# Moving a chunk's last scores and statistics up among the PV matmuls, and filling TensorE's wait for the next keys with unused matmuls

## The chip, the cores and the metric

One core of one Trainium2 chip (trn2). The metric is the device time of one execution in microseconds. Nearly everything here is a matter of one or two microseconds in 1386, so times are given as medians with all runs' range, and differences only where kernels ran in the same rounds on the same chip.

## The reference

Two decode attentions of one query token, batch 4, 32 query heads, head size 128, bf16. A is grouped (8 key heads) over the last 2048 positions; B has 32 key heads and reads all 8192.

```python
def _B_ref(x, k_cache, v_cache, wq, wo):                 # k_cache, v_cache: (4, 32, 8192, 128)
    q = (x @ wq).reshape(B, Sq, H, Dh).transpose(0, 2, 1, 3)
    scores = jnp.einsum("bhqd,bhkd->bhqk", q, k_cache) * (Dh ** -0.5)
    p = _softmax(scores, axis=-1)
    o = jnp.einsum("bhqk,bhkd->bhqd", p, v_cache)
    return o.transpose(0, 2, 1, 3).reshape(B, Sq, H * Dh) @ wo
# A the same on k_cache[:, :, Sk - W:], W = 2048, heads repeated 4 times; the results are concatenated
```

Each key and value is used once: 587 MB have to come from HBM.

## The kernel before

The work is cut into 72 chunks: 8 of A, then 64 of B ("second-half chunks"; 4 MB of keys and 4 MB of values each). For each chunk TensorE transposes the keys (groups of 8 tiles, `tr`), VectorE and ScalarE copy them to SBUF (`kt`), TensorE multiplies them with the query (`sc`). While it then does PV (probabilities times values, `po`) of the *previous* chunk, the last scores and the softmax statistics of this one (`ms`) are put in between:

```python
        def values_part(c, nxt):          # c: chunk whose PV is done; nxt: chunk whose keys just came
            ch = chunks[nxt]
            late = list(range(ch["s_last"] + 1 - SLAG, ch["s_last"] + 1))
            todo = {2: lambda: emit_S(late[0]), 5: lambda: scores_last(nxt)}
            if ch["ab"] == 1:
                todo[10] = lambda: stats_gmax(nxt)
                todo[14] = lambda: stats_exp(nxt)
            ...
            for g in range(16):
                if c is not None and g < chunks[c]["NG"]:
                    emit_pv(c, g)         # 8 matmuls
                    ...
                if g in todo:
                    todo[g]()
        ...
        for c in range(NC):
            keys_part(c)                  # transposes and scores of chunk c
            ...
            values_part(c - 1 if c else None, c)
        sch.mark()
        ...                               # after the last chunk's statistics: its own PV
        for g in range(chunks[NC - 1]["NG"]):
            emit_pv(NC - 1, g)
        pv_done(NC - 1)
        emit_fin(NC - 1)                  # output projection
```

A key load goes into the buffer of the chunk two before, as soon as its transposes are done; a value load into that of the chunk two before, when its PV is done. Two chunks of B make one period, and TensorE's instructions are a loop over the periods that are alike:

```python
            self.emit_ops(pe[:m[a]], eng, sems)            # straight code: all of A, the first two chunks of B
            with loop(0, b - a) as i:                      # a = 1, b = 32: 31 rounds of two chunks
                self.emit_ops(pe[m[a]:m[a + 1]], ...)
            self.emit_ops(pe[m[b]:], eng, sems)
```

## Time and profile before

| | kernel before |
|---|---|
| time, three runs | 1385.94 us median (1384.96 to 1386.25) |
| span of the profiled run | 1384.5 us |
| mean granted clock of TensorE | 0.931 |
| queue 1 (keys, values, weights) | 99.2% of 16 engines' span |
| TensorE's wait for keys of B | 169.0 us in 61 waits |
| last keys used at | 1358.65 us |

The page's first part gives busy time by engine, the third the queues; the chain goes back from the last instruction to what released it. In the views of windows the numbers after each engine are busy us and instructions, followed by the granted clock, the DMA share and GB/s.

### The profile page before, as it was taken

The page shows a single profiled execution, that of the slowest core. Times are in us where ns is not written, and L with a number is a line of the kernel's source. Part 1 is how long each engine was busy: PE and PEld are TensorE (multiplying, and loading weights), DVE is VectorE, ACT ScalarE, POOL GpSimd, SP SyncE. Part 2 cuts the span into 40 slices and gives each one's busy share as a digit, 9 for nine tenths or more (in the row PEclk, how much of TensorE's full clock was granted, in tenths as well). Part 3 has the DMA queues.
Part 4 walks back from the last instruction along what each step waited for, and adds up shares of the span by engine and source line. Part 5 has one row for each costly group of instructions (what it writes and reads, how often), then busy time and mean ns, then how long its engine had stood idle before and what let it go on. Part 6 is the DMA issues. An engine that isn't in the chain of part 4 may idle for free.

```text
span 1384.5 us, 57099 instructions
## 1 busy us (share of the span) xinstructions
PE 1173.0 (85%) x26769; PEld 1130.0 (82%) x26769; DVE 643.2 (46%) x1326; ACT 436.1 (31%) x649; POOL 4.1 (0%) x14
## 2 busy tenths in 40 slices
PE   4888888898888788988889788888898888888888
PEld 4777878897888788887889788887798888887887
DVE  1566444454444444444444444444454445444443
ACT  1554323333223322332233233332233233322332
POOL 1000000000000000000000000000000000000000
PEclk9899999999999999999999999999999999999998
DMA  9999999999999999999999999999999999999996
GB/s 400 414 417 422 426 428 430 434 425 437 427 436 427 432 430 434 429 425 436 427 436 427 435 427 436 426 428 435 429 434 430 433 427 435 428 429 432 431 434 255
DMA packets 29979, 587.80 MB, mean 425 GB/s; under 512 B 2656, under 2 KB 10864, under 8 KB 11120
## 3 DMA queue, kind: packets, MB, share of 16 engines
q1 hardware_dynamic: 29912, 587.22, 99.2%
q8 instruction: 27, 0.44, 0.1%
q14 instruction: 16, 0.13, 0.0%
q10 hardware_dynamic: 24, 0.01, 0.0%
HBM read 587.21 MB, written 0.01 MB: 424 GB/s over the span
## 4 chain that ended last, share of the span: by engine, by line
DMA 66%; PE 31%; DVE 1%; issue 1%; ACT 0%; SPq 0%; ACTq 0%; DVEq 0%
DMA kv<-in_B_k_cache_dram 64%; PE tr L321 19%; PE sc L323 9%; DMA kv<-in_B_wq_dram 2%; PE fin L323 2%; PE po L323 1%; PE ms L323 1%; DVE sA L430 1%; DVE kt L383 0%; DVE rm L439 0%; DVE sA L428 0%; ACT pba L493 0%; PE ms L321 0%; ACT kt L381 0%; ACT pbb L478 0%
## 5 line engine op out<-in xcount | busy, mean ns | idle before, releaser
L321 PE MATMUL tr<-identb,kv 128*128 128x128 bf16 x8704 | 702.7, 231 | 171.7 <-DMA kv<-in_B_k_cache_dram 169.0
L383 DVE COPY kt<-tr 128x1024 bf16<-128x1024 bf16 x736 | 502.6, 691 | 484.5 <-PE tr L321 480.4
L321 PEld LDWEIGHTS tr<-identb,kv 128*128 128x128 bf16 x8704 | 557.7, 105 | 197.4 <-issue 128.6
L381 ACT ACTIVATE kt<-tr 128x1024 bf16<-128x1024 bf16 x352 | 360.2, 1024 | 638.1 <-PE tr L321 635.0
L323 PE MATMUL sc<-qb,kt 128*128 128x64 bf16 x8192 | 424.6, 197 | 1.7 <-issue 1.5
L323 PEld LDWEIGHTS sc<-qb,kt 128*128 128x128 bf16 x8192 | 350.8, 101 | 3.9 <-issue 1.6
L323 PE MATMUL po<-pbb,kv 128*128 128x64 bf16 (+1 forms) x8192 | 289.9, 192 | 5.5 <-issue 5.5
L323 PEld LDWEIGHTS po<-pbb,kv 128*128 128x128 bf16 x8192 | 263.3, 97 | 7.6 <-issue 5.8
L478 ACT ACTIVATE pbb<-sc,negb 64x128 bf16<-64x128 f32 x128 | 51.2, 400 | 296.8 <-DVE negb L468 296.0
L444 DVE TENSOR_REDUCE rm<-sc 64x1 f32<-64x128 f32 x128 | 37.0, 289 | 94.2 <-PE sc L323 93.3
L456 DVE TENSOR_REDUCE gm<-ms 1x2 f32<-1x128 f32 (+1 forms) x72 | 20.1, 279 | 44.6 <-PE ms L321 44.5
L468 DVE COPY negb<-ms 128x1 f32<-128x1 f32 (+1 forms) x72 | 11.4, 159 | 55.4 <-PE ms L323 55.4
L323 PE MATMUL sc<-qs,kt 128*128 128x64 bf16 (+3 forms) x512 | 26.6, 198 | 10.8 <-DVE kt L383 10.5
L323 PEld LDWEIGHTS sc<-qs,kt 128*128 128x128 bf16 x512 | 21.8, 102 | 13.2 <-DVE kt L383 11.8
L323 PE MATMUL ms<-identf,gx 1*128 1x1 f32 (+1 forms) x144 | 27.8, 260 | 0.6 <-DVE gx L460 0.6
L323 PEld LDWEIGHTS ms<-identf,gx 1*128 1x128 f32 (+1 forms) x144 | 21.7, 188 | 4.9 <-DVE gx L460 0.8
L478 ACT ACTIVATION_READ_ACCUMULATOR pbb<-sc,negb 64x1 f32 x128 | 23.7, 185 | 0.0
L321 PE MATMUL ms<-identf,rm 128*1 128x128 f32 (+1 forms) x72 | 19.8, 275 | 0.2 <-DVE rm L444 0.2
L323 PE MATMUL fin<-wos,oz 128*4 128x512 bf16 x64 | 19.5, 386 | 0.3 <-DVE oz L542 0.3
L323 PE MATMUL po<-pba,kv 128*128 128x64 bf16 x512 | 18.9, 193 | 0.0
L460 DVE TENSOR_SCALAR gx<-gm 1x128 f32<-1x128 f32 (+1 forms) x72 | 15.9, 221 | 2.5
L323 PEld LDWEIGHTS po<-pba,kv 128*128 128x128 bf16 x512 | 16.6, 98 | 0.0
(47 smaller groups left out, 155.5 us busy)
## 6 DMA issues: line engine op xcount, KB each, us to landing
kv<-in_B_k_cache_dram SPq DMA_DIRECT2D x64, 4096.0 KB, 27.7
kv<-in_B_v_cache_dram SPq DMA_DIRECT2D x63, 4096.0 KB, 32.5
kv<-in_A_k_cache_dram SPq DMA_DIRECT2D x8, 2048.0 KB, 27.4
kv<-in_A_v_cache_dram SPq DMA_DIRECT2D x8, 2048.0 KB, 26.6
kv<-in_A_wq_dram SPq DMA_DIRECT2D x1, 4096.0 KB, 12.3
kv<-in_B_wq_dram SPq DMA_DIRECT2D x1, 4096.0 KB, 27.3
wor<-in_A_wo_dram SPq DMA_DIRECT2D x8, 512.0 KB, 23.6
wor<-in_B_wo_dram SPq DMA_DIRECT2D x8, 512.0 KB, 33.6
```

What stands on the lines that cost most here:

```text
L321: emit = lambda e: e.transpose(o, l, r)
L323: emit = lambda e: e.matmul(o, l, r, start=start, stop=stop)
L381: sch.add("act", lambda e: e.activation(dst, src, ACTF.Copy), waits=waits, key=("ev", s))
L383: sch.add("dve", lambda e: e.tensor_copy(dst, src), waits=waits, key=("ev", s))
L430: emit = lambda e, src=src, b=b: e.scalar_tensor_tensor(out=t, in0=src, scalar=mk[:, b:b + 1], in1=t, op0=ALU.mult, op1=ALU.add)
L444: sch.add("dve", lambda e, src=src, pp=pp: e.tensor_reduce(out=rm[pp, m, 0:1], in_=src, axis=AX.X, op=ALU.max), waits=[("S", ch["s_last"]) ...
L456: sch.add("dve", lambda e: e.tensor_reduce(out=gm[0:C, m, 0:U], in_=src, axis=AX.X, op=ALU.max), waits=[("trm", c)], key=("gmax", c))
L460: sch.add("dve", lambda e: e.tensor_scalar(out=dst, in0=gv, scalar1=-scale, scalar2=None, op0=ALU.mult), waits=[("gmax", c)], key=("gx", c))
L468: sch.add("dve", lambda e: e.tensor_copy(negb[:, m, 0:C], ms[:, col:col + C]), waits=[("bc", c)], key=("negb", c))
L478: sch.add("act", lambda e, src=src, pp=pp, n=n, u=u: e.activation(pbv[pp, :, u], src, ACTF.Exp, bias=negb[pp, m, 0:1], scale=scale, accum_ ...
```

## The change

It moves the last scores and statistics of a chunk earlier among the PV matmuls, adds eight matmuls of 512 columns whose result nobody reads after each PV of a B chunk, to keep TensorE's clock up while it waits for keys, and lets the very last PV use 64 columns (62 of them unused) instead of 2.

```diff
-                n = NW if c < NC - 1 else UC
+                n = NW
...
+        def keep_busy():
+            o = tr[:, (NTB // TG - 2) % NTRB, :].bitcast(F32)
+            for i in range(8):
+                pe_mm(o, identb[:, :], kt[:, NKT - 1, 0:512])
...
-            todo = {2: lambda: emit_S(late[0]), 5: lambda: scores_last(nxt)}
+            todo = {1: lambda: emit_S(late[0]), 3: lambda: scores_last(nxt)}
             if ch["ab"] == 1:
-                todo[10] = lambda: stats_gmax(nxt)
-                todo[14] = lambda: stats_exp(nxt)
+                todo[7] = lambda: stats_gmax(nxt)
+                todo[11] = lambda: stats_exp(nxt)
...                                        # at the end of values_part
+            if ch["ab"] == 1:
+                keep_busy()
```

## The prediction

> **What bounds the kernel now.** I read the page from the totals down: the busy shares, the DMA queues, the chain that ended last, and only then the waits. TensorE is busy 85% of the span and loads weights 82%, which looks like a bound; the queues say otherwise.
>
> ```profile
> span 1384.5 us, 57099 instructions
> PE 1173.0 (85%) x26769; PEld 1130.0 (82%) x26769; DVE 643.2 (46%) x1326; ACT 436.1 (31%) x649; POOL 4.1 (0%) x14
> DMA packets 29979, 587.80 MB, mean 425 GB/s; under 512 B 2656, under 2 KB 10864, under 8 KB 11120
> q1 hardware_dynamic: 29912, 587.22, 99.2%
> DMA 66%; PE 31%; DVE 1%; issue 1%; ACT 0%; SPq 0%; ACTq 0%; DVEq 0%
> kv<-in_B_k_cache_dram SPq DMA_DIRECT2D x64, 4096.0 KB, 27.7
> ```
>
> Queue 1 keeps all 16 DMA engines occupied 99.2% of the span; 587 MB of keys and values have to come through it, at 425 GB/s on average. The chain names DMA for two thirds; its 31% of PE is the time from a chunk's keys landing to the release of their buffer, after which the next key load is issued. That could be a loop in which a faster TensorE issues loads sooner and ends sooner. The last line above says that it isn't: a 4096 KB load takes, at the 430 GB/s of the steady slices, 4.19 MB / 430 = 9.8 us of all engines, but lands 27.7 us after issue. So 27.7 - 9.8 = about 18 us of it is queueing behind loads already issued. A key load could be issued up to 18 us later or any amount sooner and land at the same moment.
>
> The waits agree: TensorE waits for keys, 169 us in all, and the store of issued work never runs dry.
>
> ```profile
> PE tr L321 <- DMA kv<-in_B_k_cache_dram: 169.0, 61, 6.0
> PEld tr L321 <- issue: 128.6, 71, 6.1
> 626.00:630.00 4.00, 0.00 (x0) 0.00 (x0) 0.00 (x0) 0.29 (x2) 0.00 (x0) 0.87 0.95 410
> 630.00:634.00 4.00, 3.51 (x38) 3.52 (x39) 1.38 (x2) 0.73 (x1) 0.00 (x0) 0.50 0.95 410
> 634.00:638.00 4.00, 4.00 (x74) 4.00 (x73) 2.48 (x5) 1.31 (x2) 0.00 (x0) 0.78 1.12 483
> ```
>
> 169 / 61 = 2.8 us of waiting per chunk; a wait of some 5 us (625.5 to 630.5) alternates with one of 2.2. In the last three lines, windows from the middle of the run, the column before the DMA share is the granted clock: after the long wait the transposes start at 0.50 [...]. That is what the filler matmuls are meant to prevent.
>
> One stretch is not covered by DMA: the end. This is the chain there, start and duration in us:
>
> ```profile
> 1330.88 27.72 DMA kv<-in_B_k_cache_dram
> 1358.65 2.10 PE tr L321 x24
> ...
> 1371.47 0.71 PE po L323 x24
> ...
> 1377.46 3.27 PE po L323 x128
> 1381.04 1.03 PE fin L323 x2
> 1382.09 0.68 DVE outsb L571
> ```
>
> The last keys land at 1358.65. From there TensorE works almost without pause: 16 groups of transposes and scores to 1371.3, PV of the chunk before (with the last scores and statistics between) to 1376.2, a 0.9 us wait for the exponentials, the last 128 PV matmuls, the output projection, the cast, the store. The last value piece was issued at about 1337.7 and landed 40.1 us later, at 1377.8. So after the last keys the end is set by TensorE, not by DMA, and only these 26 us can change.
>
> [...] between 1356.0 and 1359.4 TensorE was busy for 1.01 of 3.40 us and the next 3.4 us were granted 0.50. [...] 2 matmuls of 512 columns in 0.52 us and 4 in 0.96 at full clock, 240 to 260 ns each with their change of weights[...]. [...]
>
> **The change, part by part.**
> 1. *Scores and statistics earlier.* For each chunk the last two score groups go in after 2 and 4 of the 16 PV groups (before: 3 and 6), the two statistics matmuls after 8 and 12 (before: 11 and 15). Nothing is added. The exponentials are started when 32 instead of 8 PV matmuls are still to come: 24 x 29 ns (0.70 us for 24 in the chain) = 0.7 us sooner against the end of PV. The first moved score group now needs its keys 0.47 us after PV begins. ScalarE's eviction (1.02 us) that it waits for ends 0.34 us after PV begins in the last chunk (1370.60 + 1.02 against 1371.28), so no new wait, or one of under 0.1 us.
> 2. *Eight matmuls of 512 columns after each PV* of the 64 second-half chunks: [...] In 63 of 64 they lie in the wait for keys (5 or 2.2 us); where a wait is shorter than 1.8 us the transposes start up to 1.8 us late, one tenth of the 18 us that a key load has to spare. Worth on the path: 0. They remove part of the half-clock stretches: [...] I expect the mean granted clock to rise from 0.931 to 0.95 to 0.99. That shortens TensorE's work by tens of us, which turn into longer waits for keys. Worth on the path: 0.
> 3. *The end.* (a) Half clock after the last keys: 1358.65 to 1371.3 took 12.65 us; the same stretch of a chunk at full clock, 609.46 to 620.55, took 11.09. The filler covers 1356.2 to 1358.0, so the clock should hold: -1.55. (b) PV with scores and statistics, 4.9 us as before: 0. (c) Between this PV and the last one stood 0.9 us of waiting for the exponentials. They would now be ready some 0.3 us after PV ends (0.7 sooner than the roughly 1.0 of before), but the last chunk's filler stands in front: 1.8 in place of 0.9: +0.9. (d) The last 128 PV matmuls have 64 columns in place of 2: 128 x 29 ns = 3.73 in place of 3.27: +0.45. (e) With 2 columns the clock fell to 0.50 at 1380, and the output projection ran at it, 1.03 us; [...] at full clock it is 0.52: -0.5. Sum: -1.55 + 0.9 + 0.45 - 0.5 = -0.7 us. By then all value pieces are in: with (a) and (c) the last PV starts near 1376.7 and reaches its last 16 tiles near 1380, after 1377.8.
> 4. *The first eight chunks* only get the earlier scores. The chain runs through TensorE and VectorE there until 89 us, but the loads are issued ahead and wait in the queue (their issue takes up to 5.5 us, pushed back), so a gain of at most 8 x 0.47 = 3.8 us in TensorE's work ends in its first wait for keys, at 119 us. Worth on the path: 0.
>
> **Rivals.** *The wait removed is real time.* A mean clock of 0.931 with only 1.0 and 0.5 granted means (1 - 0.931) / 0.5 = 14% of the span, 191 us, at half clock. If that set the pace, the work in it could take up to 95 us less, several per cent. For it speaks only TensorE's 85%; against it the 99.2% of queue 1 and the 18 us of queueing. It would give 1300 to 1350; I give it next to nothing. *The fillers delay the keys.* If TensorE came to lie at its bound, 1.8 us per chunk over 63 chunks would add up to 115 us (+8%). Against it: the mean wait is 2.8 us, the fillers give clock back, and lateness doesn't add up while every wait for keys isn't used up. Even if they held no clock at all, 2.8 - 1.8 = 1.0 us of wait is left. *Only the end moves, and to the worse.* If the filler doesn't hold the clock, (a) and (e) fall away and the end is 0.9 + 0.45 = 1.35 us longer: 1387.3. This is the likeliest way to be wrong, and still +0.1%. *A better end:* if all gains come and the fillers cost less, at most about 1.5 us less, since the last values land at 1377.8: 1384.4.
>
> **Range and chances.** 1385.94 - 0.7 = 1385.2 us. The three runs before spread over 1.3 us, and the end's parts can be off by one; 1383.8 to 1386.8. Everything at stake lies within 0.3%, so within 2% has nearly the whole chance.
>
> **What would show it.** Right: queue 1 still at about 99%, 425 GB/s, mean wait of TensorE for keys cut by roughly 1.8 us less what the clock gives back, the time from issue to landing of keys still 27 to 28 us, clock at 0.95 or above, the last keys landing at 1358 to 1359, the stretch to the first PV of 11.1 us, 1.8 us of filler before the last sums. Wrong: key loads landing soon after issue (a queue that ran dry), TensorE without waits for keys, or DMA at another rate than 430 GB/s in the steady slices, which would move the whole by more than the end can.

The marked cuts take out what no trace or run of this case showed of the hardware: a rule for the clock, one for a matmul's time, a bound on the loads' rate, and the working of a filler's time that rested on the second. No term of the sum is among them: it came to -1.55 + 0.9 + 0.45 - 0.5 = -0.7 us. But the 1.8 us of eight fillers, in the +0.9 and elsewhere, is my estimate; by the output projections in the trace (the "2 matmuls of 512 columns in 0.52 us and 4 in 0.96") eight would be 1.9. That the clock would be full in (e) was expected, not shown. At clock 0.50 the kernel before took 2.74 us for 24 transposes (at 630.49 us); at full clock the changed kernel took 1.51 (at 1359.16). "Only 1.0 and 0.5 granted" is what the clock's records in the trace of the kernel before hold, 43 stretches of each.

## The result, and the profile after

| | before | after |
|---|---|---|
| time, six runs each, same rounds | 1385.49 us (1384.87 to 1386.31) | 1386.57 us (1386.24 to 1388.14) |
| ratio | | 1.001, 95% interval 0.9997 to 1.0023 |

A ratio is the mean time of one kernel's runs over that of the other's of the same rounds, so not quite the ratio of the medians. Here 0.7 us less was expected and about 1 us more was measured: small, of the size of noise in one comparison, but it came back in two more (1.0012 with an interval of 0.9999 to 1.0026, and 1.0019 with 1.0005 to 1.0033). Only the last is clear of 1 by itself; three on one side make it real.

The page of the changed kernel answers to the prediction's first fence:

```profile
span 1384.2 us, 58059 instructions
PE 1229.5 (89%) x27217; PEld 1122.2 (81%) x27281; DVE 641.2 (46%) x1326; ACT 435.5 (31%) x649; POOL 4.1 (0%) x14
q1 hardware_dynamic: 29912, 587.22, 99.3%
DMA 62%; PE 35%; issue 1%; DVE 1%; ACT 0%; SPq 0%; ACTq 0%; DVEq 0%
kv<-in_B_k_cache_dram SPq DMA_DIRECT2D x64, 4096.0 KB, 28.1
```

As expected as far as it goes: queue 1 is as full as before, a key load lands 28 us after issue, TensorE is busier. The waits for keys shrank too, from 169.0 us to this:

```profile
PE tr L321 <- DMA kv<-in_B_k_cache_dram: 106.4, 54, 6.7
```

The chain at the end of the changed kernel (start, duration, work; `tr L323` are the fillers):

```profile
1359.16 1.51 PE tr L321 x24
...
1370.44 0.47 PE po L323 x16
...
1375.24 1.67 PE tr L323 x7
1377.03 3.78 PE po L323 x128
1381.12 0.61 PE fin L323 x2
1381.75 0.68 DVE outsb L571
```

The transposes are warm, that is, at full clock (24 in 1.51 us at a granted 1.00, in place of 2.10 at 0.50). From the last keys to the end it is 1384.2 - 1359.16 = 25.0 us in place of 25.85: 0.8 us less, where the prediction had 0.7. The end kept its word in this run. But the last keys were used at 1359.16, half a microsecond later than before, and this profiled run, at 1386.24 us, is the fastest of the six. The profiled run of the kernel before, at 1386.58, is slower than all six of its timed runs. So the two traces flatter the change; what they show of a loss is the lateness of the loads.

It is found in a stretch that the 40 slices of the page already hint at. Between 160 and 230 us, the kernel before and then the changed kernel:

```profile
160.00:230.00 70.00, 62.42 (x1432) 60.53 (x1430) 34.86 (x68) 23.21 (x32) 0.00 (x0) 0.94 1.00 427
```

```profile
160.00:230.00 70.00, 60.69 (x1259) 55.38 (x1260) 29.92 (x61) 19.09 (x28) 0.00 (x0) 0.93 1.00 423
```

The last column is GB/s: 4 less over 70 us is 0.7 us of loading lost. TensorE's busy time hardly differs, but it got through fewer instructions in that stretch (x1259 against x1432, some of them fillers; a chunk has about 390): it is about half a chunk behind. What put it behind is in the next two fences, TensorE's timeline around 159 us, first before, then after (start, duration, operation, in brackets the idle time ahead of it and what ended it):

```profile
155.54 0.41 PE L323 MATMUL po<-pbb,kv 128*128 128x64 bf16 x8
158.57 2.74 PE L321 MATMUL tr<-identb,kv 128*128 128x128 bf16 x24 [2.62 <-DMA kv<-in_B_k_cache_dram]
```

```profile
155.44 1.08 PE L323 MATMUL po<-pbb,kv 128*128 128x64 bf16 x31
159.21 0.19 PE L323 MATMUL po<-pbb,kv 128*128 128x64 bf16 x1 [2.68 <-issue]
159.45 1.67 PE L323 MATMUL tr<-kt,identb 128*128 128x512 bf16 x7
165.58 2.74 PE L321 MATMUL tr<-identb,kv 128*128 128x128 bf16 x24 [4.46 <-issue]
```

This is where the program enters its loop. Before, there is one pause of 2.6 us, under which the keys arrive. After, TensorE stops for 2.7 us with one PV matmul of 32 left, does it and the fillers, and stops again for 4.5 us; "issue" says that nothing the profile sees held it. The keys had long been there (their last packet landed at 157.8): the transposes begin 7 us later than before. The DMA view knows more: queue 8, which carries instructions, moves one packet in each of the two pauses, here in 156.5 to 159.2 and in 161.1 to 165.6 us:

```profile
q8 instruction: 1, 0.02, 2.5%
q8 instruction: 1, 0.02, 1.5%
```

By the trace's packets they landed at 157.91 and 163.80. The load queue shows the consequence, before and after:

```profile
149.39 0.33 SPq L291 DMA_DIRECT2D kv<-in_B_k_cache_dram  x1
...
170.46 0.33 SPq L291 DMA_DIRECT2D kv<-in_B_k_cache_dram  x1
```

```profile
150.89 0.33 SPq L291 DMA_DIRECT2D kv<-in_B_k_cache_dram  x1
...
178.72 0.33 SPq L291 DMA_DIRECT2D kv<-in_B_k_cache_dram  x1
```

28 us between two key loads in place of 21. Adding up what had been issued and what had landed by each issue (from the trace's issues and packets, divided by 430 GB/s), the loads queued at a key load fall from 13.9 us to 6.0, 5.1 and 4.0 in the next three chunks; in the kernel before they are 11.3 us or more there. At 4 us the queue is empty for single engines: near 220 us they have no packet for 4.7 us in sum, as much as 0.29 us of all 16, which happens in no trace of the kernel before, and the waits for keys return only at 316 us.

### The profile page after: what moved, and what is told of

It reads as the page before. It is cut to its first block, busy times and chain, and to the rows that moved or that the text cites. A ratio compares the mean times of both kernels' runs of the same rounds, so it can differ in the third digit from the quotient of the medians.

```text
span 1384.2 us, 58059 instructions
## 1 busy us (share of the span) xinstructions
PE 1229.5 (89%) x27217; PEld 1122.2 (81%) x27281; DVE 641.2 (46%) x1326; ACT 435.5 (31%) x649; POOL 4.1 (0%) x14
## 4 chain that ended last, share of the span: by engine, by line
DMA 62%; PE 35%; issue 1%; DVE 1%; ACT 0%; SPq 0%; ACTq 0%; DVEq 0%
DMA kv<-in_B_k_cache_dram 58%; PE tr L321 20%; PE sc L323 9%; PE po L323 3%; DMA kv<-in_A_k_cache_dram 2%; DMA kv<-in_B_wq_dram 2%; PE tr L323 1%; PE ms L323 1%; PE fin L323 1%; DVE sA L430 0%; ACT kt L381 0%; DVE kt L383 0%; ACT pba L493 0%; PE ms L321 0%; DVE outsb L571 0%
## 5 line engine op out<-in xcount | busy, mean ns | idle before, releaser
L321 PE MATMUL tr<-identb,kv 128*128 128x128 bf16 x8704 | 661.6, 223 | 119.7 <-DMA kv<-in_B_k_cache_dram 106.4
L321 PEld LDWEIGHTS tr<-identb,kv 128*128 128x128 bf16 x8704 | 521.8, 100 | 166.9 <-issue 80.9
L323 PE MATMUL sc<-qb,kt 128*128 128x64 bf16 x8192 | 412.0, 194 | 1.1 <-issue 0.9
L323 PEld LDWEIGHTS sc<-qb,kt 128*128 128x128 bf16 x8192 | 335.9, 99 | 5.1 <-issue 1.1
L323 PE MATMUL po<-pbb,kv 128*128 128x64 bf16 x8192 | 290.6, 192 | 6.9 <-issue 6.8
L323 PEld LDWEIGHTS po<-pbb,kv 128*128 128x128 bf16 x8192 | 263.9, 97 | 6.2 <-issue 4.5
L323 PE MATMUL tr<-kt,identb 128*128 128x512 bf16 x448 | 107.6, 380 | 3.7 <-issue 0.4
L323 PEld LDWEIGHTS tr<-kt,identb 128*128 128x128 bf16 x512 | 45.7, 98 | 48.7 <-issue 3.6
L323 PE MATMUL sc<-qs,kt 128*128 128x64 bf16 (+3 forms) x512 | 26.2, 196 | 3.4 <-DVE kt L383 3.1
L323 PE MATMUL ms<-identf,gx 1*128 1x1 f32 (+1 forms) x144 | 27.3, 257 | 1.4 <-DVE gx L460 1.4
L323 PEld LDWEIGHTS ms<-identf,gx 1*128 1x128 f32 (+1 forms) x144 | 21.2, 183 | 5.7 <-DVE gx L460 2.1
L323 PEld LDWEIGHTS sc<-qs,kt 128*128 128x128 bf16 x512 | 21.0, 101 | 5.8 <-DVE kt L383 3.9
L542 DVE TENSOR_TENSOR oz<-po,rz 128x8 bf16<-128x8 f32 x32 | 5.3, 166 | 33.3 <-PE po L323 33.3
L323 PE MATMUL fin<-wos,oz 128*4 128x512 bf16 x64 | 19.2, 381 | 0.3 <-DVE oz L542 0.3
```

The lines of the kernel that those rows point to most:

```text
L321: emit = lambda e: e.transpose(o, l, r)
L323: emit = lambda e: e.matmul(o, l, r, start=start, stop=stop)
L542: sch.add("dve", lambda e: e.tensor_tensor(out=o, in0=i0, in1=i1, op=ALU.mult), waits=[("rinv", c), ("pv", c)] + ([("fin", c - 2)] if c >= ...
```

## The experiments

Kernels are compared only within the same rounds. All outputs are right.

**Noise, the change again, each half alone.** a1 is the kernel before, a2 the changed kernel, unedited.

> The kernel before once more, as a measure of noise. All theories: ratio 1.000, within 0.0005 of it. If it comes out 0.0007 or more from 1, the measured 1.001 of the change is of the size of noise.

> The changed kernel once more. Theory A (the extra 1 us is chance in the loads, the end is 0.7 us shorter): ratio 0.9995 plus or minus 0.0007. Theory B (the fillers slow the loads by about 2 us over the run): 1.0008, every time. Theory C (the moved scores change the loads of the first chunks): 1.0008 as well.

a3, the fillers alone:

```diff
 # kernel before
+        def keep_busy(): ...
+            if ch["ab"] == 1:
+                keep_busy()
```

> The kernel before with the eight fillers alone, scores and statistics at their old places, last PV with 2 columns. The end: clock held, -1.55; filler of 1.8 in front of the last PV in place of a wait of 0.9, +0.9: about -0.65 us. Theory A: ratio 0.9995. Theory B: loads 1.9 us later, in sum +1.2 us, 1.0009. Theory C: 0.9995. Clock 0.97 in all.

a4, the change without them:

```diff
 # changed kernel
-            if ch["ab"] == 1:
-                keep_busy()
```

> The changed kernel without the fillers. The end: cold transposes stay, the wait before the last PV shrinks from 0.9 to 0.3, the wider last PV +0.45, the projection at full clock -0.5: about -0.7 us. Theory A: ratio 0.9995. Theory B: 0.9995, no cost in the loads. Theory C: +1.2 us, 1.0009. Clock 0.93 in all.

| run | median us (range) | ratio | GB/s, 160 to 230 us | first use of the last keys, us | from there to the end, us |
|---|---|---|---|---|---|
| a1 before | 1386.14 (1384.75 to 1387.29) | 0.9997 | 428 | 1358.33 | 27.0 |
| a2 after | 1387.49 (1385.98 to 1388.99) | 1.0012 | 423 | 1358.88 | 26.5 |
| a3 fillers only | 1387.19 (1385.51 to 1388.25) | 1.0009 | 416 | 1360.66 | 24.4 |
| a4 moves only | 1384.23 (1384.14 to 1385.91) | 0.9993 | 428 | 1358.56 | 23.7 |

(before: 1386.20 us, 9 runs; single ratios have intervals of about 0.0014 to either side.) By these times alone chance (A) isn't excluded, as each interval reaches past 1. With the traces it is: the lost bandwidth is there in each of these traces with fillers and in none without. The moved scores (C) show no cost; alone they gain 1.2 us by the means.

a2 shows something else. Its loads cost it little, but its end took 26.5 us: the last transposes ran at half clock (24 in 2.12 us) in spite of the fillers. More on that below.

**Where the fillers hurt.** My theory was that fillers hurt only in the stretch in which TensorE still fetches its instructions, and there in each chunk.

b1, b2 and b3:

```diff
-            if ch["ab"] == 1:
+            if nxt >= NCA + 6:                  # b1: late
+            if NCA <= nxt < NCA + 6:            # b2: early
+            if NCA + 6 <= nxt < NC - 1:         # b3: late, and none before the last PV
                 keep_busy()
```

> The changed kernel with fillers only from the seventh second-half chunk on (58 of 64), so none in the stretch where TensorE still fetches its instructions. Theory B1 (the loads lose time only near 200 us, where fetch stalls plus fillers put TensorE so far behind that the queue of loads runs dry): no idle DMA engines between 20 and 1340 us, 10 us or more of loads queued at every key load, last keys at 1357.5 to 1358.8, ratio 0.9990 to 0.9996. Theory B2 (every filler costs the loads a little, by contention): 58/64 of the cost stays, ratio 1.0010.

> The complement: fillers only for the first six second-half chunks. Theory B1: the cost stays, DMA engines idle 0.3 us or more near 220 us, queue down to 2 to 5 us; end as without fillers; ratio 1.0003 to 1.0010. Theory B2: 6/64 of the cost, ratio 0.9994, nothing idle.

> As the late fillers, and none before the last PV. The end: clock held for the last transposes (-1.5 against the kernel before) and no filler of 1.8 us in front of the last PV, 0.3 of waiting in its place: -1.55 -0.6 +0.45 -0.5 = -2.2 us. Theory B1: ratio 0.9984, the fastest of all. Theory B2: 1.0000.

b4 is the changed kernel with the loop found from the seventh mark on, so that ten more chunks are straight code:

```diff
-        for a in range(len(self.marks) - 1):
+        for a in range(6, len(self.marks) - 1):
```

> The changed kernel, the same instructions, but the loop on TensorE begins ten chunks later, so those ten chunks are fetched as straight code too. Theory B1: each such chunk takes about 22 us in place of 19.4, so after the queue is dry every further one costs about 2.5 us: +20 us or more against the kernel before, ratio 1.012 to 1.020, DMA engines idle from 200 to 420 us. Theory B2: the matmuls are the same, ratio 1.001.

| run | median us (range) | ratio | idle DMA, as us of all 16 engines |
|---|---|---|---|
| b1 late | 1387.35 (1386.63 to 1387.64) | 1.0008 | 1.6, from 260 to 320 us |
| b2 early | 1386.70 (1385.73 to 1388.60) | 1.0005 | 0.7, from 260 to 320 us |
| b3 late, not last | 1388.65 (1387.06 to 1390.30) | 1.0014 | 1.7, from 240 to 320 us |
| b4 long straight code | 1393.75 (1391.57 to 1402.74) | 1.0063 | 7.5, from 380 to 420 us |

(before: 1386.29 us, 11 runs.) My theory fell with b1: with no filler before 230 us the queue ran dry all the same, only later. But the same contention in every chunk (B2) fares no better: nothing is lost in the 1000 us in which most fillers stand. The traces say what the three have in common. Skipping fillers in the first chunks makes those periods unlike the later ones, so the loop begins two rounds later, at 230 to 245 us; and it is at the *entry of the loop* that all of them lose. In b1 the pauses there are 1.6 and 6.0 us, and loading runs at 413 GB/s between 240 and 310 us where the kernel before has 428. b2 has no filler after its entry; its queue had already sunk to 9.4 us under the fillers before it. b4 settles where. Ten chunks of straight code with fillers bring the queued loads slowly from 12 to 5.5 us, and then the entry, at 376 us, takes them to nothing. And at the old place, where b4 runs the same instructions as the changed kernel without entering a loop, the first pause is still there and the second is gone (first three lines; the fourth is b4's own entry):

```profile
158.16 0.19 PE L323 MATMUL po<-pbb,kv 128*128 128x64 bf16 x1 [1.62 <-issue]
158.40 3.04 PE L323 MATMUL tr<-kt,identb 128*128 128x512 bf16 x7
161.23 1.86 PE L321 MATMUL tr<-identb,kv 128*128 128x128 bf16 x24
...
376.13 2.74 PE L321 MATMUL tr<-identb,kv 128*128 128x128 bf16 x24 [5.69 <-issue]
```

Its cost, about 9 us with a spread of 11, is less than half of the 20 that I expected, as straight code alone was only mildly slower there (6.5 us of queue in ten chunks, fillers included).

**The entry's place in a fetch block.** Why is the entry bad in one kernel and harmless in another with nearly the same code? The packets of queue 8 have 16384 bytes, and they are TensorE's instructions: in the changed kernel the queue moves none between 209 us, when TensorE's loop has gone round once, and 1379 us, when it has left it. How many instructions one holds can be counted in the traces: TensorE's pauses for "issue" in the loop's first round, at 177.81, 192.41 and 198.85 us in the kernel before, stand 511 and 256 of its instructions apart, those at 185.41 and 204.77 us in the changed kernel 767, all within one of a multiple of 256. So I take a packet as a block of 256. Two chunks' fillers come before the entry: 16 matmuls, with their weight loads 32 instructions. In the changed kernel the first pause comes 18 instructions ahead of the entry (1 PV matmul and 8 fillers, two each). So a block boundary should lie 18 instructions before the entry, and without the 32 it would lie 14 behind it. The suspicion: just past a boundary, one waits for a block, uses 18 instructions of it, jumps, and waits again.

That can be tested by tiny matmuls in TensorE's idle first 13 us (in c2 and c3 half of them stand after `emit_xT`), which change little but the position of all later code: with 64 or more the first transposes start 1.1 to 1.3 us later, but the first of B start at 119.2 to 119.8 us with and without them.

```diff
+            for i in range(n):      # c1: 16, on the kernel before; c2 and c3: 112, on the changed one
+                pe_mm(tr[:, 0, :].bitcast(F32)[0:8, 0:8], identb[:, 0:8], identb[:, 0:8], ...)
         emit_xT()
```

> The kernel before with 16 tiny matmuls (32 instructions) in TensorE's idle start, which moves the entry of its loop by as many instructions as the fillers of two chunks do. Theory D1 (where the loop entry lies against the 16 KB blocks in which instructions are fetched decides): two stalls in a row at the entry, one before the last PV matmuls of about 2 us and one of 4 us or more after, as in the changed kernel; the first transposes of that chunk at 162 us or later (158.6 in the kernel before); loads queued at the next key load fall from 14 to 7 to 10 us, nothing runs dry because there are no fillers; ratio 0.9995 to 1.0005. Theory D2 (fillers alone do it): as the kernel before, 158 us.

> The changed kernel with 112 tiny matmuls (224 instructions) in TensorE's idle start: with the 32 of the fillers 256, one whole fetch block, so the loop entry lies in its block as in the kernel before. D1: one stall at the entry, first transposes there at 161 to 163 us in place of 165.6, 7 us or more of loads queued at every key load, no DMA engine idle between 20 and 1340 us, last keys at 1357.5 to 1358.8; end -0.7: ratio 0.9990 to 0.9998 where the changed kernel had 1.0012. D2: nothing changes, 1.0012.

c3 is c2 with `if ch["ab"] == 1 and nxt < NC - 1:` ahead of the fillers; c4 is a4 again.

> As the one before, and no filler in front of the last PV: the end another 1.3 us shorter, -2.0 in all. D1: ratio 0.9982 to 0.9990, the fastest. D2: 1.0002.

> The moved scores and statistics without any filler once more (0.9993 before): 0.9988 to 0.9996. If it is as fast as the one before it, the fillers are worth nothing even where they do no harm.

The entry in c1, the kernel before moved by 32 instructions:

```profile
156.93 0.16 PE L323 MATMUL ms<-identf,gx 1*128 1x1 f32 x1 [2.04 <-issue]
157.02 0.41 PE L323 MATMUL po<-pbb,kv 128*128 128x64 bf16 x8
163.25 1.03 PE L321 MATMUL tr<-identb,kv 128*128 128x128 bf16 x8 [5.82 <-issue]
```

and in c2, the changed kernel moved by 224:

```profile
157.18 1.67 PE L323 MATMUL tr<-kt,identb 128*128 128x512 bf16 x7
160.89 1.61 PE L321 MATMUL tr<-identb,kv 128*128 128x128 bf16 x24 [2.03 <-issue]
```

32 instructions without a filler among them give the kernel before the changed kernel's two pauses; 224 more take them from the changed kernel.

| run | median us (range) | ratio | fewest us of loads queued after the entry | GB/s, 160 to 230 us |
|---|---|---|---|---|
| c1 before + 32 | 1386.45 (1385.18 to 1387.15) | 1.0001 | 7.0 | 428 |
| c2 after + 224 | 1385.58 (1385.39 to 1385.77) | 0.9996 | 9.0 | 429 |
| c3 the same, no last filler | 1386.46 (1385.11 to 1387.42) | 1.0003 | 9.1 | 430 |
| c4 moves only | 1384.30 (1384.16 to 1386.01) | 0.9993 | 11.1 | 429 |

(before: 1386.31 us, 9 runs.) c1 also says why the bad entry alone costs nothing: without fillers the queue falls to 8.6 and 7.0 us and is back at 12.6 two chunks later, where the changed kernel sinks to 4.0 and is at 8.8 two chunks later. Every trace whose queue ran dry has both, stops for fetching (at the entry, in b4 to a small part in the straight code too) and fillers before or after them.

The traces show why the place matters. In the stretch to 300 us the packets of queue 8 never follow each other in less than 5.6 us, which fits an entry waiting longest when it needs a block soon after the last one came. The pause at the entry was 3.1 to 7.2 us where the pause before it lies 18 to 26 instructions back (eight traces), 2.8 us with about 122 in b2, 2.7 us with about 146 in d4 (below), and 1.9 to 2.0 us in c2 and d3, where 18 and the move by 224 make 242. In each of these, TensorE goes on 1.8 or 1.9 us after the packet has landed.

c3 missed. Leaving out one filler makes the last period unlike the others, so the loop ends a round early and its last chunks are fetched as straight code: its trace has a pause of 1.05 us for "issue" inside the end, at 1371.85, and seven packets of queue 8 after 1345 us for c2's one. b3 has the same fault, with 2.39 us at 1355.10. Neither says what the last filler costs.

**Side by side, another place, and fillers that stand in nobody's way.** d2 is the changed kernel, d3 is c2. d4 has 64 tiny matmuls (128 instructions). d1 has the fillers at the head of the key parts, so that the loop keeps its 31 rounds and none stands in front of the last PV, with 120 tiny matmuls to put the entry in its old place:

```diff
-            if ch["ab"] == 1:                  # end of values_part
-                keep_busy()
...
             if c >= NCA and (c - NCA) % 2 == 0:
                 sch.mark()
+            if c > NCA:                        # head of keys_part
+                keep_busy()
```

> The changed kernel with the fillers at the head of each key part instead of at the end of each value part, so that none stands in front of the last PV and the loop still covers all chunks, and with 120 tiny matmuls at the start so that the loop entry lies in its fetch block as in the kernel before. Alignment theory: no DMA engine idle between 20 and 1340 us, last keys near 1358.5, from them to the end 23.7 us; ratio 0.9985 to 0.9992, all runs within 0.7 us of each other. If the fillers hold no clock in the last wait: 25 us, ratio 0.9993 as without fillers.

> The changed kernel beside the others on one chip: 1.0008 to 1.0014, scattered over 2 us, DMA engines idle near 220 us.

> The changed kernel with its loop entry moved by 224 instructions, once more: 0.9993 to 0.9999, all runs within 0.7 us; nothing idle. It must lie below the changed kernel of the same call in every run but perhaps one, or the alignment theory is not shown in the time.

> The changed kernel with its loop entry moved by 128 instructions, some 146 past the boundary of a fetch block in place of 18. Alignment theory: the block before is used for longer, so no two stalls in a row of more than 4 us together with 2; first transposes of that chunk at 161 to 164 us, 6 us or more of loads queued; ratio 0.9994 to 1.0004. If any move of the entry helps because of the tiny matmuls themselves: as with 224, 160.9 us.

| run | median us (range) | ratio | transposes after the entry at, us | fewest us queued | GB/s, 160 to 230 us |
|---|---|---|---|---|---|
| d2 after | 1388.21 (1386.67 to 1389.46) | 1.0019 | 165.90 | 3.7 | 419 |
| d3 after + 224 | 1385.67 (1385.45 to 1386.77) | 1.0001 | 160.94 | 9.0 | 428 |
| d4 after + 128 | 1385.73 (1385.64 to 1387.41) | 1.0005 | 163.47 | 5.3 | 426 |
| d1 fillers in key parts | 1384.49 (1384.28 to 1385.74) | 0.9992 | 160.37 | 11.2 | 427 |

(before: 1385.25 us, 9 runs.) The same instructions, moved by 224, are faster by 2.4 us in the mean (1385.85 against 1388.22), and the ranges of five runs hardly touch. A move by 128 lands in between at the entry and in the queue, so it is the place that counts and not the padding; its queue and its ratio fell just outside of what I had expected (6 us or more, at most 1.0004). Of the other expectations, d3's ratio was to be below 1 and its runs within 0.7 us (1.0001 and 1.3 us came), and d1's runs within 0.7 us with an end of 23.7 us, or 25 if the fillers hold no clock (1.5 and 25.2).

How much of the 2.4 us is the loads? In the two profiled runs, 1387.60 and 1385.74 us, the last keys are used 0.4 us later in d2 (1359.06 against 1358.67); the other 1.5 us is the end, 26.5 us against 25.0. So in these traces the loads are the smaller part, and a second thing was at work, in a2 and d2: in the last wait for keys the clock fell although the fillers were there. The clock's records of the two kernels' traces are stretches at 1.0 or 0.5, each but the last a whole multiple of 3.413 us long. Windows of about that length, of d2:

```profile
1356.00:1359.40 3.40, 1.40 (x11) 0.64 (x10) 0.00 (x0) 0.00 (x0) 0.00 (x0) 1.00 1.01 434
1359.40:1362.80 3.40, 3.40 (x43) 3.40 (x40) 1.38 (x2) 1.02 (x1) 0.00 (x0) 0.51 0.94 405
```

and of the profiled run of the changed kernel, where it held:

```profile
1355.40:1358.80 3.40, 1.69 (x8) 0.59 (x6) 0.24 (x2) 0.12 (x2) 0.00 (x0) 1.00 1.05 453
1358.80:1362.20 3.40, 3.04 (x64) 2.98 (x64) 2.03 (x4) 1.02 (x1) 0.00 (x0) 1.00 0.94 405
```

The wait that the fillers leave over is 2.0 us in both. If it falls wholly into one window, TensorE was busy for 1.40 of its 3.40 us and the next window is granted half clock; if it is split between two windows, 1.69 of 3.40 in the first is enough to keep it. Where the windows lie differs between traces of the same program: by the clock's own records one begins at 1358.8 us in the trace of the changed kernel, at 1359.4 in d2 and at 1359.6 in a2. In the trace of the changed kernel, cut into windows by these records, all 13 changes from full to half clock after 100 us follow a window with 1.40 us or less of TensorE's work, and all 347 windows that stay at full clock one with 1.43 or more. In the other traces some changes (of all 18, 40 of 448) follow more than 1.42 us of work; why was not looked into. d1's profiled run was unlucky as well (24 transposes in 2.42 us, end 25.2, 1385.69 us); three of its five runs are at 1384.3 to 1384.5. The moves without fillers show the same two levels in both lots, three runs at 1384.1 to 1384.3 and two at 1385.7 to 1386.0, and their two traces, both of the lower level, have warm last transposes with no filler at all.

So fillers that do no harm are worth nothing here: 0.9992 with them (d1), 0.9993 twice without (a4, c4). They were run at other times.

## Why the prediction was wrong

- *DMA bounds the kernel, and TensorE's stretches in mid-run are worth nothing.* Right. TensorE waited 63 us less for keys, the mean granted clock of the profiled run rose from 0.931 to 0.978, and queue 1 stayed at 99%.
- *Step 2, "the transposes start up to 1.8 us late, one tenth of the 18 us that a key load has to spare. ... Worth on the path: 0."* This is the step that failed in every trace of the changed kernel: the cost that it set at nothing. In the traces the last keys are used 0.4 to 0.55 us later (1359.16 for 1358.65; a2 against a1; d2 against d3). Three terms were wrong. The spare time is less than 18 us: counted from issues and packets, the median of the steady key loads of the kernel before is 13 us queued; 27.7 - 9.8 also counts that the 16 engines don't finish a load together (first and last 6.9 us apart in the median). The lateness was not 1.8 us, but about 7 at one place, the loop entry, where the 32 added instructions of the fillers put the entry 18 instructions past the first pause, which I take for the boundary of a fetch block. And the prediction's sentence against its second rival, that "lateness doesn't add up while every wait for keys isn't used up", was true of the steady state and overlooked that after such a stop there are no waits: the fillers lengthen chunks that are already late, the queue falls to 4 us, and engines go idle. Moving the entry by 224 instructions removes the second pause, the lost bandwidth and the idle engines (c2, d3); fillers without moves bring them (a3); a moved entry without fillers brings the stop but not the loss (c1). The sign that I had named for being wrong, a queue that ran dry, came, if only for 0.29 us.
- *Step 3, the end.* Its size was right where the clock held, -0.8 us for -0.7, term by term: the stretch to PV 11.12 for 12.66 us (-1.54; predicted -1.55), from there to the last PV 6.61 for 6.01 (+0.6; predicted +0.9), the last PV 3.90 for 3.39 (+0.5; +0.45), the projection 0.59 for 1.01 (-0.4; -0.5). But (a), "the clock should hold", is a chance and not a fact: this step failed in a2 and d2, two of the three traces, and cost 1.5 us there, more than the loads. Nor need the cold end of both traces of before (25.85 us, and 27.0 in a1) be the rule: four of nine runs in the last lot are at 1384.75 to 1384.87, 1.7 us under the profiled run. That fits an end with a warm clock, but no trace of such a run of the kernel before was taken; it is argued, not shown. Against such a run the filler before the last PV only costs.
- *Steps 1 and 4.* Step 1 was right: the moves need no new wait worth naming and seem to be the useful part of the change, 0.9993 twice (each interval reaching past 1). Step 4 wasn't tested by itself.
- *Readings and sums.* A filler takes 239 ns (7 recorded ones in 1.67 us), so eight are 1.9 us, not 1.8. The waits of 5 and 2.2 us don't alternate: the next five are 1.3, 3.5, 2.2, 3.5 and 2.6 us. Pushed back key loads of the first chunks take up to 18.0 us to issue, not 5.5. None of this changes the sum. The line of 128.6 us that I quoted, weight loads waiting for "issue" in the kernel before, is not instruction fetch, as one might think: 102.9 us of it lie between 300 and 1300 us, where queue 8 moves nothing, and are the waits for keys seen from the weight loads. The fetch stood in a small line beside it, PV matmuls waiting 5.5 us in 3 times for "issue".
- *Rivals.* "Real time" was rightly dropped. "The fillers delay the keys" had the direction, at one place and for half a microsecond instead of 115. "Only the end moves, and to the worse" came nearest in size (+1.35); its first half, a clock that doesn't hold, came true in a2 and d2, its second (e) in none of the three traces, where the projection took 0.59 us, and it left out the loads. None of them named instruction fetch.
- *What stays open.* How the loss of a single timed run splits between late loads and a cold end: only profiled runs leave a trace. If the lower of two levels of times is the warm end, the changed kernel has it at 1386.0 to 1386.7 us (seven of its 16 runs) and the kernel moved by 224 at 1385.4 to 1385.8, which would make the late loads worth 0.6 to 0.9 us; that is argued, not shown. Also why the clock held in nine of ten runs, by their times, of the kernel moved by 224 and less often in the others; if the windows' position is free, that was luck.

## What to carry to other kernels

Instructions that only fill a wait are still instructions: in a kernel with a loop they move the code, and where the loop was entered 18 instructions past the pause for a block, the engine stopped twice (2.7 and 4.5 us in the changed kernel, 2.1 and 4.1 in d2; moved by 224, one pause of 1.9 to 2.0 us); look for "issue" pauses around loop entries and exits, before and after, and try padding in idle time. A deep queue of loads forgave a late buffer here where there were waits in which to catch up (c1: from 7.0 us queued to 12.6 two chunks later), and fillers used up just these (the changed kernel: from 4.0 to 8.8). Before you compare traces that differ by a microsecond, see where each profiled run lies among its kernel's times.
